# Sliding-window attention beside a gated feed-forward layer: the values' weights on ScalarE's queue, the order of early loads, and chunk 3's softmax in one group

## The chip, the cores and the metric

The kernel runs on one core of a Trainium2 chip. A core has TensorE (matmuls, PE in the profile; PEld is its loading of weights), VectorE (DVE), ScalarE (ACT), GpSimd (POOL) and SyncE (SP). SyncE, ScalarE and GpSimd can issue transfers, each on a queue of its own. The metric is the device time in microseconds (us) of one execution; lower is better.

## The reference

x has 2048 rows of 640 bf16 numbers. A layer normalization (no learned parameters) gives xn; two branches read it and their outputs are added to x:

```
xn = (x - mean(x)) / sqrt(var(x) + 1e-5)
# A: 32 heads of 20; each position s sees s, s-2, ..., s-14 (8 keys, dilation 2)
q, k, v = split(xn @ wqkv)
attn    = softmax(q . k[s - 2w] * 20**-0.5  over w = 0..7, masked where s - 2w < 0)
A       = (sum over w of attn[w] * v[s - 2w]) @ wo
# B: gated, without a nonlinearity
B       = ((xn @ w_gate) * (xn @ w_up)) @ w_down      # 640 -> 1536 -> 640
out     = x + A + B
```

## The kernel before

**Tiles and chunks.** The 2048 rows are 16 tiles of 128 rows, in four chunks of 512 rows. For each chunk the kernel makes xnT (the normalized x transposed, so that TensorE can contract over the 640 columns), q, k and v, the attention, the gate and up products, and the down projection. TensorE does the projections (line 464 by tiles of 128 rows, in chunk 0 while x is still arriving; line 500 by chunks), the gate and up products (L746), and down with the output projection of the attention (L809 for wd, L812 for wo). VectorE does the attention itself: products of q and k (L555), sums over the 20 numbers of a head in the `fold` steps (L530, L535), then, after TensorE has added up the last partial sums into logits with a matrix of ones and zeros (`logits`, L582, PSUM tile `pl`), the softmax (`softmax`: maximum L618, subtraction L622, sum L640, reciprocal L643, scaling L649; the exponential is ScalarE's, L632), and the weighted sum over v (`av`: products L698, sums L708 and L706, output tile oT). The softmax's weights go to device memory (aD, L658) and come back spread over the partitions (aE, four transfers a chunk, L666), each issued on SyncE's queue. VectorE also multiplies gate by up (hT, L763).

**Groups of the softmax.** `GR = (1, 1, 1, 2)` says in how many groups of positions each chunk's logits, softmax, store and spreading are done. In one group a chunk has eight logits matmuls, and its softmax works on 128x1024 numbers. Chunk 3 has two groups: four logits matmuls and half-sized operations for each, a store and four spreading transfers for each, and two half-sized products of L698 for each tile.

**Tiles 0 to 7.** Tiles 0 to 2 are transposed by TensorE (L385) and copied out by ScalarE (L390); from tile 3 on a transposing transfer on SyncE's queue does it (`transposes`, L379). Normalization of tiles 0 to 7: VectorE takes the statistics (L253, L259), GpSimd a power of -1/2 (L267, rstd), VectorE applies them (L272), in place in the x tile. There are five x buffers, so x of tile t+5 can be loaded only when tile t has been transposed. x of tile 8 is loaded by GpSimd's queue, right behind tile 3's transpose:

```
        if t + 5 < W:
            X[t + 5] = load((11.0, 11.5, 14.2)[t], load_x(t + 5), [a])
        elif t == 3 or 8 <= t < NT - 5:
            X[t + 5] = add("POOL", 6.0, load_x(t + 5, nc.gpsimd), [a], occ=0.45, kb=160)
```

**Weights.** wq comes in three loads on ScalarE's queue (lines 235 to 237), followed by x of tile 3. wk and wv come on SyncE's queue (L185). The order on SyncE's queue before: x0, x1, x2, wk, x4, x5, x6, x7, tile 3's transpose, wv, the transposes of tiles 4 to 7, wg, x9 to x12, wu, wd, wo. x8 is on GpSimd's queue, ahead of which GpSimd waits for tile 3's transpose.

**What sets the order.** Every piece of work is a `Step` in a `Plan`, with an engine, a planned cost, how long it occupies its engine (`occ`), and the steps that it depends on. `Plan.order` is a list scheduler: on each engine it takes, of the steps that are ready, the one whose latest start is earliest, and it writes the instructions in that order. `PACE` scales the planned costs of an engine. Dependences given to `add` and `load` steer the plan only; on the chip an instruction waits for data and buffers alone, and each engine runs its instructions in the order written. `load` makes a step on SyncE's queue behind the load before it, with an earliest planned landing. TensorE's steps are chained one behind the other in the order of the program text (`pe_main`), each waiting for the PSUM bank used six steps before; only the logits are slotted in where the plan has them ready (a `margin` of 0.9 in chunk 0, 1 elsewhere).

Of the kernel before, what the change touches and what calls it, by code (L numbers as in the profile page):

```python
# [9 lines left out]
ACT = mybir.ActivationFunctionType  # L10
# [22 lines left out]
class Plan:  # L33
# [1 line left out]

    LAG = 0.06
    RAW = 0.116
    PACE = {"DVE": 1.03, "ACT": 1.0}
    INORDER = ("DVE", "PE", "ACT")

    def __init__(self):
# [2 lines left out]
    def add(self, eng, cost, fn, deps=(), occ=None, after=(), kb=0):  # L44
        k = self.PACE.get(eng, 1.0)
        s = Step(eng, cost * k, fn, deps, None if occ is None else occ * k, after)
        s.kb = kb
        s.pace = k
        s.idx = len(self.steps)
        self.steps.append(s)  # L50
        return s
# [60 lines left out]
def kernel(  # L112
# [11 lines left out]
    nc = tc.nc  # L124
# [3 lines left out]
    S, D = x_flat.shape  # L128
# [3 lines left out]
    W = 8  # L132
# [6 lines left out]
    NT = S // P  # L139
# [16 lines left out]
    wv = const.tile([P, KT, D], BF, name="wv")  # L156
# [10 lines left out]
    add = plan.add  # L167
    T = {}

    def new(key, shape, dtype, tag, bufs, pool=None):  # L170
        t = (pool or sb).tile(shape, dtype, name=tag, tag=tag, bufs=bufs)
        T[key] = t
        return t


    def load_x(t, eng=None):
        def fn():
            x = new(("x", t), [P, D], BF, "x", 5)
            (eng or nc.sync).dma_start(out=x[:], in_=x_flat[t * P : (t + 1) * P, :])
        return fn  # L180

    X = {}

    def wload(dst, src, eng=None):
        return lambda: (eng or nc.sync).dma_start(out=dst[:], in_=src.rearrange("(i p) f -> p i f", p=P))  # L185
# [10 lines left out]
    def load(at, fn, deps=()):  # L196
        s = chain[0] = add("SP", 2.0, fn, deps, occ=0.45, after=[chain[0]])
        s.floor = at
        return s

    def part(r, lo, hi):
        src = A_wqkv[lo * P : hi * P, r * D : (r + 1) * D].rearrange("(i p) f -> p i f", p=P)
        return lambda: nc.scalar.dma_start(out=WT[r][:, lo:hi, :], in_=src)  # L203
# [31 lines left out]
    WP = []  # L235
    for lo, hi, at in ((0, 1, 4.4), (1, 3, 5.1), (3, KT, 5.5)):
        WP.append(add("ACT", at, part(0, lo, hi), [C0], occ=0.48, after=WP[-1:]))
    X[3] = add("ACT", 5.2, load_x(3, nc.scalar), occ=0.45, after=[WP[2]])
    TB = add("ACT", 1.6, table, after=[X[3]])

    def warm():
# [34 lines left out]
    XT, TT, GL, RS = {}, {}, {}, {}  # L276
# [3 lines left out]
    def behind(s, a):  # L280
        s.after.append(a)
        s.deps.append(a)
        plan.steps.remove(s)
        plan.steps.append(s)
# [5 lines left out]
    def st_in(t, g, d=None):  # L290
        return inline("DVE", 0.48, ln_stats(t, g), [d or X[t]], 0.395)
# [5 lines left out]
    def apply_in(t):  # L297
        XT[t] = inline("DVE", 0.443, ln_apply(t), [RS[t]], 0.4)
# [57 lines left out]
    def pe_main(cost, fn, deps=(), banks=1):  # L356
        nonlocal main
        waits = []
        for k in range(banks):
            if len(ring) + k >= 6:  # L360
                waits.append(ring[len(ring) + k - 6])
        main = add("PE", cost + 0.165, fn, [main, *waits, *deps], occ=cost)
        return main
# [6 lines left out]
    def transposes(t):  # L370
        c, q = divmod(t, CH)

        def slot():
            if q == 0:
                new(("xnT", c), [P, KT, CS], BF, "xnT", XB)

        def dma():
            slot()
            nc.sync.dma_start_transpose(out=T["xnT", c][:, :, q * P : (q + 1) * P], in_=T["x", t][:])  # L379

        def piece(g0, g1, n):
            def pe():
                ps = new(("pst", t, n), [P, KT, P], BF, "ps", 6, psum)
                for g in range(g0, g1):
                    nc.tensor.transpose(ps[:, g, :], T["x", t][:, g * P : (g + 1) * P], ident[:])  # L385

            def ev():
                if n == 0:
                    slot()
                nc.scalar.copy(T["xnT", c][:, g0:g1, q * P : (q + 1) * P], T["pst", t, n][:, g0:g1, :])  # L390
            return pe, ev

        if t in PIECES:
            for n, (g0, g1) in enumerate(PIECES[t]):
                p, e = piece(g0, g1, n)
                w = g1 - g0
                a = pe_main(w * 0.056, p, [XT.get((t, n), XT[t])])
                a = add("ACT", 0.16 + w * P / 1200, e, [a, TT.get(t)], occ=0.07 + w * P / 1200)
                TT[t] = a
                TX.setdefault(t, []).append((g0, g1, a))  # L400
                ring.append(a)
            if t:
                behind(PV[t - 1][0], TT[t])
        else:
            if c < 2:
                a = TT[t] = chain[0] = add("SP", 3.0, dma, [XT[t]], occ=1.28, after=[chain[0]])
            else:
                a = TT[t] = add("SP", 2.8, dma, [XT[t], GP.get(c - XB)], occ=1.28, kb=200)
        if t + 5 < W:
            X[t + 5] = load((11.0, 11.5, 14.2)[t], load_x(t + 5), [a])  # L410
        elif t == 3 or 8 <= t < NT - 5:
            X[t + 5] = add("POOL", 6.0, load_x(t + 5, nc.gpsimd), [a], occ=0.45, kb=160)

    LL = {}
    GR = (1, 1, 1, 2)
    PV = {}
    R = {}
    PROJ = ("q", "k", "v")
# [12 lines left out]
    def halo(c, r):  # L431
# [10 lines left out]
        else:  # L442
            w = LL.get((c - 2, GR[c - 2] - 1)) if r == 1 else O16.get(CH * (c - 1) - 1)
            HALOCP[r, c] = add("ACT", 0.25, fn, [w, *R[r, c - 1]])
# [10 lines left out]
    def tile_part(r, t, n, g0, g1, deps):  # L455
        c, q = divmod(t, CH)
        j0, j1 = JS[n]

        def pe():
            if g0 == 0:  # L460
                new(("psv", r, t, n), [P, 512], F32, "ps", 6, psum)
            for j in range(j0, j1):
                for i in range(g0, g1):
                    nc.tensor.matmul(T["psv", r, t, n][:, (j - j0) * P : (j - j0 + 1) * P], lhsT=lhs(r, i, j),  # L464
                                     rhs=T["xnT", c][:, i, q * P : (q + 1) * P], start=(i == 0 and j == j0), stop=(i == KT - 1),
                                     skip_group_check=True)

        ws = WQ[: (1, 2, 2, 3, 3)[g1 - 1]] if r == 0 else WW[r]
        return pe_main((g1 - g0) * (j1 - j0) * 0.056, pe, [*deps, *ws], banks=1 if g0 == 0 else 0)
# [16 lines left out]
    def proj_tile(r, t, ns=(0, 1)):  # L486
        for n in ns:
            a = None
            for g0, g1, x in TX[t] if n == 0 and t in TX else [(0, KT, TT[t])]:
                a = tile_part(r, t, n, g0, g1, [x])  # L490
            tile_evict(r, t, n, a)

    def proj(c, r, lo=0, n=CS):
        for j in range(KT):
# [11 lines left out]
            ts = range(c * CH + lo // P, c * CH + (lo + n) // P)  # L506
            old = LL.get((c - 2, GR[c - 2] - 1)) if r < 2 else O16.get(CH * (c - 1) - 1)
            a = pe_main(KT * (n / 2400 + 0.0027), pe, [*WW[r], *[TT[t] for t in ts], old])
            e = add("ACT", 0.16 + n / 1200, ev, [a, HALOCP.get((r, c)), R.get((r, c - 2), [None])[0]], occ=0.07 + n / 1200)
# [54 lines left out]
    before = {}  # L564
    order = [(c, g) for c in range(NCH) for g in range(GR[c])]
    for a, b in zip(order, order[1:]):
        before[b] = a

    def logits(c, g):
        n = (c, g)  # L570
        E = CS // 4 // GR[c]

        def lg():
            if g == 0:
                new(("lps", c), [P, 2 * CS], F32, "pl", 1, psum)
            l = T["lps", c][:, g * W * E : (g + 1) * W * E].rearrange("p (w s) -> p w s", w=W)
            sets = 3 - GR[c]
            for b in range(sets):
# [5 lines left out]

        took = 0.2 + 0.2195 * 2 / GR[c]
        folds = [FO[4 * c + u] for u in range(4) if GR[c] == 1 or u // 2 == g]
# [276 lines left out]
    a = st_in(0, 0)  # L863
    a = st_in(0, 1, a)
    aggr_in(0, a)
    a = st_in(1, 0)
    a = st_in(1, 1, a)
# [8 lines left out]
    halo(0, 1)  # L876
    halo(0, 2)
    transposes(0)
    a0 = [None, None]
    for k, (g0, g1, x) in enumerate(TX[0]):  # L880
        for n in range(2):
            if k == 2 and n == 1:
                a = st_in(2, 0, None)
                a = st_in(2, 1, a)
                apply_in(1)
                transposes(1)
                WV = None
            a0[n] = tile_part(0, 0, n, g0, g1, [x])
            if k == 2:
                tile_evict(0, 0, n, a0[n])  # L890
    aggr_in(2, a)
    proj_tile(0, 1, (0,))
    a = st_in(3, 0)
    a = st_in(3, 1, a)
# [4 lines left out]
    proj_tile(0, 2, (0,))  # L899
    apply_in(3)  # L900
    transposes(3)
    WV = load(14.6, wload(wv, A_wqkv[:, 2 * D : 3 * D]))
    WW = (WP, [WK], [WV])
    proj_tile(0, 2, (1,))
    proj(0, 1, 0, 3 * P)
    proj_tile(0, 3)
# [4 lines left out]
        ln(t)  # L911
        transposes(t)
    WL["g"] = load(28.5, wload(wg, B_w_gate))
    for t in range(9, 13):
        X[t] = load(30.0, load_x(t), [TT[t - 5]])
    WL["u"] = load(36.0, wload(wu, B_w_up))
    proj(0, 2)
# [68 lines left out]
```

## Time and profile before

| | us |
|---|---|
| median of 3 runs | 258.23 (257.91 to 258.67) |
| profiled execution | 258.23 |
| its span, first to last instruction | 256.5 |
| TensorE busy | 251.8 (98%) |
| VectorE busy | 223.5 (87%) |
| ScalarE busy | 129.1 (50%) |
| GpSimd busy | 41.8 (16%) |
| transfers | 24.65 MB, 96 GB/s over the span |

The granted TensorE clock was 1.000. A row of the time-ordered view has: start in us, length in us, engine, line, operation, output tile and input tile, number of instructions, and in brackets the idle time of the engine just before and what ended it. Rows merge neighbouring instructions of one kind. Engine names with a q (SPq, ACTq) are the issuing of transfers; a transfer's own time to landing stands in the view of transfers, as the last number of a line. A row of the chain that ended last has: start, length, and the work that was on the chain then.

### The profile page before, as it was taken

To read this page: it belongs to the slowest core of one execution; us is meant where nothing else is said; L and a number is where in the kernel's file an instruction comes from. 1 tells how busy PE (TensorE), PEld (TensorE's weight loads), DVE (VectorE), ACT (ScalarE), POOL (GpSimd) and SP (SyncE) were. 2 spreads that over 40 slices of the span, in tenths; PEclk is the share of its full clock that TensorE was granted. 3 is DMA by queue.
4 is the path that set the end of the run, shared out by engine and by line. 5 is a ranking of instruction groups with operands and counts; after the bars stand their busy time and mean duration, and the time that the engine had idled before them with its cause. 6 is when DMAs were issued, how large, how long until landed. Compare 5 with 4: busy or idle time off the path is not lost.

```text
span 256.5 us, 3786 instructions
## 1 busy us (share of the span) xinstructions
PE 251.8 (98%) x1481; PEld 141.4 (55%) x1481; DVE 223.5 (87%) x273; ACT 129.1 (50%) x250; POOL 41.8 (16%) x61
## 2 busy tenths in 40 slices
PE   7999999999999999999999999999999999999995
PEld 2885554444456775444455766444457754445763
DVE  5769999997999999999999999799999999994011
ACT  2656689786589164655554114545542135554100
POOL 2432000411100711004100112000293120000110
PEclk9999999999999999999999999999999999999999
DMA  6895999058500278051400132520005534000221
GB/s 216 259 192 105 399 391 335 3 152 179 157 0 3 27 95 85 7 191 44 170 0 0 17 38 27 145 88 0 0 3 127 130 31 102 23 0 3 24 27 51
DMA packets 21953, 24.65 MB, mean 96 GB/s; under 512 B 10032, under 2 KB 18352, under 8 KB 21872
## 3 DMA queue, kind: packets, MB, share of 16 engines
q1 hardware_dynamic: 18672, 17.86, 24.0%
q0 software_dynamic: 2432, 5.57, 13.5%
q10 hardware_dynamic: 832, 0.98, 1.2%
q8 instruction: 11, 0.18, 0.3%
q14 instruction: 6, 0.05, 0.1%
HBM read 18.61 MB, written 5.96 MB: 96 GB/s over the span
## 4 chain that ended last, share of the span: by engine, by line
PE 96%; DMA 2%; ACTq 0%; DVE 0%; issue 0%
PE ps L746 40%; PE ps L500 23%; PE ps L809 20%; PE ps L812 8%; PE ps L464 3%; DMA wq<-in_A_wqkv_dram 2%; PE pl L582 1%; ACTq L203 0%; PE ps L385 0%; DVE x L820 0%; DVE gs L214 0%; DVE mhalf L216 0%; DVE dm L189 0%
## 5 line engine op out<-in xcount | busy, mean ns | idle before, releaser
L746 PE MATMUL ps<-xnT,wg 128*128 128x512 bf16 x240 | 59.7, 379 | 0.0
L746 PE MATMUL ps<-xnT,wu 128*128 128x512 bf16 x240 | 59.6, 379 | 0.0
L809 PE MATMUL ps<-wd,hT 128*128 128x320 bf16 (+2 forms) x384 | 57.4, 299 | 0.0
L698 DVE TENSOR_TENSOR av<-v,aE 128x5120 bf16<-128x5120 bf16 (+1 forms) x20 | 45.6, 2286 | 3.7 <-DMA aE<-aD 3.7
L809 PEld LDWEIGHTS <-hT 128*128 128x128 bf16 x384 | 37.0, 98 | 16.3 <-issue 0.7
L555 DVE TENSOR_TENSOR pw<-qk 128x2560 bf16<-128x2560 bf16 x28 | 40.8, 1485 | 0.1
L746 PEld LDWEIGHTS <-wu 128*128 128x128 bf16 x240 | 23.5, 98 | 28.3
L746 PEld LDWEIGHTS <-wg 128*128 128x128 bf16 x240 | 23.3, 98 | 28.1 <-issue 0.5
L751 ACT CAST us<-ps 128x512 bf16<-128x512 f32 x48 | 28.1, 585 | 21.2 <-PE ps L746 20.2
L751 ACT CAST gs<-ps 128x512 bf16<-128x512 f32 x48 | 28.1, 585 | 20.4 <-PE ps L746 20.3
L708 DVE TENSOR_TENSOR av<-av 128x2560 bf16<-128x2560 bf16 (+1 forms) x32 | 36.9, 1153 | 0.2
L824 ACT COPY y<-ps 128x320 f32<-128x320 f32 x28 | 11.5, 426 | 42.6 <-PE ps L812 32.7
L853 POOL DMA_DIRECT2D out_dram<-y x14 | 12.2, 871 | 105.3 <-ACT y L824 86.7
L812 PE MATMUL ps<-wo,oT 128*128 128x320 bf16 (+2 forms) x160 | 27.0, 299 | 0.0
L504 ACT CAST qk<-ps 128x512 bf16<-128x512 f32 (+1 forms) x35 | 19.9, 569 | 12.2 <-PE ps L500 12.2
L530 DVE TENSOR_TENSOR pw<-pw 128x2048 bf16<-128x2048 bf16 (+1 forms) x28 | 25.6, 951 | 0.0
L500 PE MATMUL ps<-xnT,wv 128*128 128x512 bf16 x100 | 22.3, 379 | 0.0
L763 DVE TENSOR_TENSOR hT<-gs,us 128x512 bf16<-128x512 bf16 x48 | 19.7, 417 | 2.5 <-ACT us L751 2.3
L500 PE MATMUL ps<-xnT,wk 128*128 128x512 bf16 (+1 forms) x100 | 20.9, 366 | 0.0
L812 PEld LDWEIGHTS <-oT 128*128 128x128 bf16 x160 | 15.5, 98 | 6.3
L790 POOL COPY gate<-hT 1x1 bf16<-1x1 bf16 x4 | 10.6, 2652 | 51.2 <-DVE hT L763 51.2
L500 PEld LDWEIGHTS <-wv 128*128 128x128 bf16 x100 | 11.6, 118 | 9.7 <-issue 0.4
(67 smaller groups left out, 200.8 us busy)
## 6 DMA issues: line engine op xcount, KB each, us to landing
aE<-aD SPq DMA_DIRECT2D x12, 256.0 KB, 4.0
out_dram<-y POOLq DMA_DIRECT2D x14, 160.0 KB, 3.8
wg<-in_B_w_gate_dram SPq DMA_DIRECT2D x1, 1920.0 KB, 9.1
wu<-in_B_w_up_dram SPq DMA_DIRECT2D x1, 1920.0 KB, 13.0
wd<-in_B_w_down_dram SPq DMA_DIRECT2D x1, 1920.0 KB, 17.9
out_dram<-in_A_x_dram POOLq DMA_DIRECT2D x3, 640.0 KB, 4.2
x<-in_A_x_dram SPq DMA_DIRECT2D x11, 160.0 KB, 5.3
aE<-aD SPq DMA_DIRECT2D x8, 128.0 KB, 2.6
```

Source lines behind the costliest of these rows:

```text
L500: nc.tensor.matmul(T[key][:, 0:n], lhsT=lhs(r, i, j), rhs=T["xnT", c][:, i, lo : lo + n], start=(i == 0), stop=(i == KT - 1))
L504: nc.scalar.copy(where(r, c, j, j + 1, lo, n)[:, 0, :], T[key][:, 0:n])
L530: nc.vector.tensor_tensor(w[:, :, lo:hi, :], w[:, :, lo:hi, :], w[:, :, a:b, :], ALU.add)
L555: nc.vector.tensor_tensor(o, qh, kh, ALU.mult)
L698: nc.vector.tensor_tensor(o, v, w, ALU.mult)
L708: nc.vector.tensor_tensor(v[:, 0:k], v[:, 0:k], v[:, k : 2 * k], ALU.add)
L746: nc.tensor.matmul(ps[:], lhsT=(wu if r else wg)[:, i, f * P : (f + 1) * P], rhs=T["xnT", c][:, i, :], start=(i == 0), stop=(i == KT - 1))
L751: nc.scalar.copy(s[:], T[key][:])
L763: nc.vector.tensor_tensor(h[:], T["gs", c, f][:], T["us", c, f][:], ALU.mult)
L809: nc.tensor.matmul(ps, lhsT=T["hT", c, f][:, q * P : (q + 1) * P], rhs=wd[:, f, sl], start=(f == 0), stop=(f == FT - 1 and not wo_part))
L812: nc.tensor.matmul(ps, lhsT=T["oT", t][:, g, :], rhs=wo[:, g, sl], start=False, stop=(g == KT - 1 and f1 == FT))
L853: nc.gpsimd.dma_start(out=out_flat[t * P : (t + 1) * P, :], in_=T["y", t][:], accum_op=ALU.add)
```

## The change

1. The pace of VectorE in the plan goes from 1.03 to 1.02, and the planned cost of x3's load from 5.2 to 5.0.
2. wv's load moves from SyncE's queue to ScalarE's, planned after the normalization of tile 3 (`XT[3]`).
3. On SyncE's queue x7 moves from the place behind tile 2's transpose to behind tile 3's transpose.
4. x8 moves from GpSimd's queue (behind tile 3's transpose) to SyncE's, between wg and x9.
5. Chunk 3's softmax goes in one group: `GR` is (1, 1, 1, 1).

wq's three loads stay. The order on SyncE's queue after: x0, x1, x2, wk, x4, x5, x6, tile 3's transpose, x7, the transposes of tiles 4 to 7, wg, x8 to x12, wu, wd, wo.

```diff
--- before.py
+++ after.py
@@ -35,7 +35,7 @@
 
     LAG = 0.06
     RAW = 0.116
-    PACE = {"DVE": 1.03, "ACT": 1.0}
+    PACE = {"DVE": 1.02, "ACT": 1.0}
     INORDER = ("DVE", "PE", "ACT")
 
     def __init__(self):
@@ -235,7 +235,7 @@
     WP = []
     for lo, hi, at in ((0, 1, 4.4), (1, 3, 5.1), (3, KT, 5.5)):
         WP.append(add("ACT", at, part(0, lo, hi), [C0], occ=0.48, after=WP[-1:]))
-    X[3] = add("ACT", 5.2, load_x(3, nc.scalar), occ=0.45, after=[WP[2]])
+    X[3] = add("ACT", 5.0, load_x(3, nc.scalar), occ=0.45, after=[WP[2]])
     TB = add("ACT", 1.6, table, after=[X[3]])
 
     def warm():
@@ -406,13 +406,13 @@
                 a = TT[t] = chain[0] = add("SP", 3.0, dma, [XT[t]], occ=1.28, after=[chain[0]])
             else:
                 a = TT[t] = add("SP", 2.8, dma, [XT[t], GP.get(c - XB)], occ=1.28, kb=200)
-        if t + 5 < W:
-            X[t + 5] = load((11.0, 11.5, 14.2)[t], load_x(t + 5), [a])
-        elif t == 3 or 8 <= t < NT - 5:
+        if t < 2:
+            X[t + 5] = load((11.0, 11.5)[t], load_x(t + 5), [a])
+        elif 8 <= t < NT - 5:
             X[t + 5] = add("POOL", 6.0, load_x(t + 5, nc.gpsimd), [a], occ=0.45, kb=160)
 
     LL = {}
-    GR = (1, 1, 1, 2)
+    GR = (1, 1, 1, 1)
     PV = {}
     R = {}
     PROJ = ("q", "k", "v")
@@ -884,7 +884,6 @@
                 a = st_in(2, 1, a)
                 apply_in(1)
                 transposes(1)
-                WV = None
             a0[n] = tile_part(0, 0, n, g0, g1, [x])
             if k == 2:
                 tile_evict(0, 0, n, a0[n])
@@ -899,8 +898,9 @@
     proj_tile(0, 2, (0,))
     apply_in(3)
     transposes(3)
-    WV = load(14.6, wload(wv, A_wqkv[:, 2 * D : 3 * D]))
+    WV = add("ACT", 5.4, wload(wv, A_wqkv[:, 2 * D : 3 * D], nc.scalar), [XT[3]], occ=0.48)
     WW = (WP, [WK], [WV])
+    X[7] = load(14.6, load_x(7), [TT[2]])
     proj_tile(0, 2, (1,))
     proj(0, 1, 0, 3 * P)
     proj_tile(0, 3)
@@ -911,7 +911,7 @@
         ln(t)
         transposes(t)
     WL["g"] = load(28.5, wload(wg, B_w_gate))
-    for t in range(9, 13):
+    for t in range(8, 13):
         X[t] = load(30.0, load_x(t), [TT[t - 5]])
     WL["u"] = load(36.0, wload(wu, B_w_up))
     proj(0, 2)
```

## The prediction

> **What bounds the kernel now.** I read the page first, then the chain that ended last, then the time-ordered rows from 5 to 45 us, where most of the edits lie, and the VectorE rows from 160 us on, for chunk 3.
>
> ```profile
> span 256.5 us, 3786 instructions
> PE 251.8 (98%) x1481; PEld 141.4 (55%) x1481; DVE 223.5 (87%) x273; ACT 129.1 (50%) x250; POOL 41.8 (16%) x61
> ...
> 2.17 5.82 DMA wq<-in_A_wqkv_dram
> ...
> 10.36 2.01 PE ps L464 x35
> 12.37 4.06 PE ps L500 x25
> 16.43 2.79 PE ps L464 x50
> 19.22 21.58 PE ps L500 x100
> 40.81 0.64 PE pl L582 x8
> ...
> 166.15 0.33 PE pl L582 x4
> ...
> 206.49 0.33 PE pl L582 x4
> ```
>
> TensorE is busy 251.8 of 256.5 us. After the last load of wq has landed (2.17 + 5.82 = 7.99) each piece of the chain starts where the one before ends, to 253.6. So any edit after 8 us can win only TensorE work that it removes, and loses one for one where it makes TensorE wait. Nothing in the diff changes the loads ahead of 8 us. The profiled execution took 258.23 us, equal to the median of the three runs: 1.73 us lie outside the span.
>
> The second thing to see is how little slack the early rows have:
>
> ```profile
> 11.11 1.31 SPq L379 DMA_TRANSPOSE xnT<-x  x1
> 12.48 1.92 SPq L185 DMA_DIRECT2D wv<-in_A_wqkv_dram  x1
> 14.50 8.47 SPq L379 DMA_TRANSPOSE xnT<-x  x4
> 15.86 0.76 POOL L179 DMA_DIRECT2D x<-in_A_x_dram  x1 [2.39 <-DMA xnT<-x]
> 16.11 1.56 PEld L464 LDWEIGHTS <-wq 128*128 128x128 bf16 x25
> 16.64 0.57 POOL L267 TENSOR_TENSOR rstd<-ve,mhalf 128x1 f32<-128x1 f32 x1
> 17.26 0.45 DVE L272 TENSOR_SCALAR x<-x,mv,rstd 128x640 bf16<-128x640 bf16 x1 [2.18 <-POOL rstd L267]
> 19.06 5.56 PE L500 MATMUL ps<-xnT,wv 128*128 128x512 bf16 x25
> 24.45 5.56 PE L500 MATMUL ps<-xnT,wq 128*128 128x512 bf16 x25
> ...
> xnT<-x SPq DMA_TRANSPOSE x1, 4.4
> ...
> wv<-in_A_wqkv_dram SPq DMA_DIRECT2D x1, 800.0 KB, 6.4
> ```
>
> The last two lines are from the view of transfers: the transpose of tile 3 lands 4.4 us after its issue (11.11 + 4.4 = 15.5) and TensorE's weights for that tile load at 16.11: slack 0.6 us. wv lands at 12.48 + 6.4 = 18.9, wanted at 19.06. The transpose of tile 7, alone at the end of its four, takes 2.6 us from 21.77 and lands at 24.4, wanted at 24.45. And GpSimd, waiting for tile 3's transpose to issue x8, holds up the rstd of tile 5 (ready at 14.28, run at 16.64) and so VectorE by 2.18 us.
>
> **wv on ScalarE's queue.** Its issue costs ScalarE 0.40 to 0.49 us (the three rows of wq). The planner places it when tile 3's normalization is planned to end (11.09 in the trace); there ScalarE has just finished copying tile 2's transposes (10.28 to 11.03). The evictions behind it slip 0.45 us; TensorE does not feel that, since six PSUM banks of 0.56 to 0.86 us each lie between an eviction and the matmul that reuses its bank, and ScalarE idles 0.33 to 0.44 us ahead of each of the next evictions. If the issue came ahead of tile 2's copies it would cost 0.45 us; I take 0. wv itself, issued 1 us sooner, lands by 11.5 + 6.4 = 17.9 at the latest row: hidden. wv has no wait of its own on the chip, since nothing used its buffer before.
>
> The price is elsewhere. Before, wv's bytes moved after the transpose of tile 3, on the same queue (from 16 to 19 us, at 300 to 385 GB/s: 2.1 us for 800 KB). Now they are in flight beside it. Rows for a transpose: alone 2.6 us; with GpSimd's accumulating store beside it 5.7 and 4.8 (issued at 93.75 and 95.07, the two ahead of them 2.6); tile 3's own, with no other data queue beside it, 4.4, because its packets on one engine came only from 14.05 to 14.75, behind a fetch of instructions that began at 12.56. Lower end 2.6: lands at 13.7, no wait. Upper end 4.4 + 2.1 = 6.5: lands at 17.6, a wait of 1.5. I take 5.4, between the two rows with another queue beside them: lands at 16.5, TensorE waits 0.3 to 0.4. The Trainium skill ("DMA: Bandwidth & Descriptors", issuing engines are not separate DMA queues) says that transfers from different issuers share the same 16 engines and interleave. The trace agrees: x tile 0, ahead of the wq loads, lands in 2.2 us, and tiles 1 and 2 beside them in 3.3 and 5.1. The same skill ("Advanced Engine Details and Errata", X-Bar transpose) gives transposes nearly the speed of plain copies, 350 to 400 GB/s; by that an estimate for tile 3's 160 KB is 0.45 us of transfer, it would be through before wv's bytes start, and the sum would lose its 0.3. The trace disagrees: tile 7's, undisturbed, moves from 22.95 to 23.75, 200 GB/s.
>
> **Tile 3's transpose ahead of x7.** Its issue waits for tile 3's normalization (ends 11.09), and x7's issue was over at 10.71; so it still starts at 11.11 and its first packets follow some 1.15 us later as tile 7's do: 0 gained. x7 is issued at 12.45 in place of 10.39 and lands 2.2 to 5.5 us later (the quickest and slowest x loads up to here), 14.7 to 18.0. VectorE reads it at 17.92 in the old order. So at worst 0.1 us later, which tile 7's transpose (slack 0.1) would hand on; I take 0. With wv gone from SP's queue, tile 4's transpose can be issued at 14.0 in place of 14.50.
>
> **x8 on SP's queue.** GpSimd is free at 14.28, so tile 5 is normalized up to 2.2 us sooner, and tiles 6 and 7 as far as x7 allows. What this moves is VectorE, not TensorE: 0 by itself, and a cushion for tile 7. x8 is now issued behind wg, at about 23.7; the x9 issued there takes 8.9 us, so x8 lands near 32.5. ScalarE reads x8 at 31.61, and would wait 0.9 with evictions queued behind it; the six banks, now of 1.08 us each, cover that. wu, behind 160 KB more (0.4 us at 400 GB/s), lands at 25.83 + 13.0 + 0.4 = 39.2; the first wu matmul is at 42.46: hidden. Its issue adds about 0.5 us on SP ahead of wu, wd and wo, inside the same 3 us.
>
> **Chunk 3 in one group.** TensorE: two groups of four logits matmuls, 0.33 + 0.33, become one of eight, 0.54 to 0.64 in the other chunks: -0.1 us, the only work removed. VectorE before and after, per operation:
>
> ```profile
> 192.16 0.68 DVE L618 TENSOR_REDUCE m<-pl 128x64 f32<-128x512 f32 x1
> ...
> 203.08 1.28 DVE L535 TENSOR_TENSOR qk<-pw 128x1024 bf16<-128x1024 bf16 x2
> ...
> 151.62 1.22 DVE L618 TENSOR_REDUCE m<-pl 128x128 f32<-128x1024 f32 x1
> ...
> 167.03 2.83 DVE L698 TENSOR_TENSOR av<-v,aE 128x5120 bf16<-128x5120 bf16 x1 [2.07 <-DMA aE<-aD]
> ```
>
> Five softmax operations cost 0.68 + 0.70 + 0.68 + 0.55 + 0.69 = 3.30 twice, 6.6, against 1.22 + 1.23 + 1.22 + 0.95 + 1.23 = 5.85; eight products of 1.48 (11.8) become four of 2.83 (11.3). VectorE saves 1.2 us, off the path. But all attention weights of the chunk now wait for its last half. The last sum (204.36) loses 3.30 of softmax and 2.89 of products in front of it, some 201.1 to 204.4; take the logits at 204.2. In chunk 2, logits to weights took 151.02 to 160.02 (9.0) and weights to first product 160.04 to 167.03 (7.0): first product at 220.2. There the four outputs followed after 6.4, 15.7, 22.0 and 25.2 us: 226.6, 235.9, 242.2, 245.4. TensorE wants them at 236.33, 241.22, 245.84 and 251.58; the least slack is 3.6 us. Cost 0; if the cover is gone, one for one beyond 3.6.
>
> **Planner numbers.** The pace of 1.02 and x3's 5.0 change only the order in which steps are written. TensorE's own order is fixed but for the logits. In chunk 1 the last sum ends at 95.34 and the logits start at 96.71, in chunk 2 at 147.49 and 151.0; in chunk 0 there is no slack (the last sum ends at 41.00, during its logits, which take 0.64 and not 0.54). I take 0; bounds -0.1 (chunk 0's 0.1 back) and +1.0 (below).
>
> **Sum.** 256.5 - 0.1 + 0.3 = 256.7, with 1.73 outside 258.4 us. A change under 0.3% (0.8 us) is about what a measurement of this kernel cannot tell from none.
>
> **Rivals.** (1) *Tile 3 pays in full.* wv and the transpose start together and the engine that was late is late by wv's share too; TensorE stands 0.9 to 1.5 us at 16.4. For it: a slack of 0.6 and 5.7 us in a neighbouring row; against it, those rows are mostly shorter than 6. It decides from a landing of 6.0 us (17.1) on: 256.5 - 0.1 + 1.2 + 1.73 = 259.3. (2) *The logits come a step too early.* The planner now takes VectorE for 1% quicker; over the 54 us before chunk 1's logits that is 0.5 us against steps of 2.3, a chance of about one in five that they move one step, to 94.4, where they wait 1.0 for the sums; chunk 0's could move by 1.08 with no slack at all: 259.2. (3) *Chunk 3's weights come late* by more than 3.6 us: 260 to 262. (4) *Faster by over 0.3%.* It needs 0.8 us; TensorE's waits on wq are 1.0 in all and no edit reaches them, the logits give 0.1 each at two places: about 257.4, for a shorter start that I can't name. (5) *The edits do nothing*: wv and tile 3 don't meet, 258.1; it lies within the forecast's own range.
>
> **How the numbers follow.** The forecast with (5), waits of 0 to 0.8 us: 0.55, its own range 258.0 to 259.0. (1) 0.24, (2) 0.11, (3) 0.06, (4) 0.04. Slower by over 0.3%: 0.24 + 0.11 + 0.06 = 0.41; same 0.55; faster 0.04. The range runs from 257.9 to 259.8: it leaves out (3), (4) and the tail of (1), under 2 in 10.
>
> **What would show it.** Tile 3's transpose lands between 15.5 and 17.6 and the first matmul on tile 3 has an idle time released by that transfer; GpSimd's rstd of tile 5 runs by 15; VectorE has no 2.18 us wait there; one group of eight logits near 204 us, VectorE's last output near 245. The prediction is wrong if the chain shows a wait on a sum ahead of logits, or on wv, tile 7's transpose or chunk 3's outputs.

## The result, and the profile after

| | before | after |
|---|---|---|
| median of 12 runs, us | 257.85 (257.31 to 260.25) | 259.57 (258.35 to 262.02) |
| profiled execution, us | 258.23 | 259.8 |
| its span, us | 256.5 | 257.7 |

The ratio of the two is 1.0070, with a 95% interval of 1.0049 to 1.0091: the change makes the kernel slower by 1.7 us. All ratios below are against the kernel before on the same chip.

The head of the page of the changed kernel and, from its fourth part, the share of the chain by engine:

```profile
span 257.7 us, 3750 instructions
...
PE 250.6 (97%) x1464; PEld 141.2 (55%) x1481; DVE 223.5 (87%) x264; ACT 128.9 (50%) x249; POOL 44.0 (17%) x60
...
PE 92%; DMA 4%; DVE 2%; issue 1%; POOL 0%; SPq 0%
```

TensorE is the bound as before, but a transfer now stands in its chain. (1464 against 1481 matmuls is no saving: 17 matmul records are missing from this trace, and the weight loads are 1481 in both.) From the chain, in order of time (start, length, what):

```profile
10.61 6.69 DMA xnT<-x
17.34 2.99 PE ps L464 x50
```

The transpose of tile 3 lands 6.69 us after its issue, and the tile's 50 matmuls begin at 17.34. The rows around it in the time-ordered view:

```profile
10.35 0.38 ACTq L185 DMA_DIRECT2D wv<-in_A_wqkv_dram  x1
10.61 1.31 SPq L379 DMA_TRANSPOSE xnT<-x  x1
11.59 4.23 PE L500 MATMUL ps<-xnT,wk 128*128 128x384 bf16 x25
12.02 0.59 SPq L179 DMA_DIRECT2D x<-in_A_x_dram  x1
14.16 0.55 POOL L267 TENSOR_TENSOR rstd<-ve,mhalf 128x1 f32<-128x1 f32 x1 [0.89 <-DVE ve L261]
17.34 1.59 PE L464 MATMUL ps<-xnT,wq 128*128 128x128 bf16 x25 [1.52 <-DMA xnT<-x]
17.79 0.89 DVE L253 BATCH_NORM_STATS2 st<-x 128x6 f32<-128x320 bf16 x2 [2.26 <-DMA x<-in_A_x_dram]
```

wv's load is issued 0.26 us ahead of the transpose, TensorE then stands 1.52 us for the transpose, and VectorE stands 2.26 us for x7. From the start of the projection with wk to tile 3, TensorE took 12.21 to 16.27 = 4.06 us before, and 11.59 to 17.34 = 5.75 us now (both in the time-ordered view): 1.69 us more, which is the whole difference of the medians (1.72). The spans differ by only 1.2 because wq's last load happened to take 5.8 us in the profiled execution of before and 4.7 in this one, so this one reached wk's projection 0.62 us sooner. The list of TensorE's waits holds no other new one: none on wv, on tile 7's transpose, on sums ahead of logits, or on chunk 3's outputs.

Why the transpose is so late is seen in the packets of the queues, in windows of half a microsecond, from the view of transfers. q10 is ScalarE's queue (wv), q1 SyncE's (here the transpose); a line gives packets, MB, and the share of 16 engines. The first window is 12.0 to 12.5, then 13.5 to 14.0 and 14.5 to 15.0:

```profile
q10 hardware_dynamic: 30, 0.04, 52.6%
...
q10 hardware_dynamic: 140, 0.18, 100.0%
...
q1 hardware_dynamic: 356, 0.09, 233.5%
q10 hardware_dynamic: 51, 0.05, 29.8%
```

From 12.0 to 14.0 q10 moves 30 + 95 + 132 + 140 = 397 packets and q1 not one. The transpose's small packets come only when wv's have nearly run out. In this trace the bytes of wv do not share with the transpose, they go ahead of it. The Trainium skill ("DMA: Bandwidth & Descriptors", issuing engines are not separate DMA queues) says that transfers of different issuers interleave. The first loads of x and wq do so in the trace of before: from 4.0 to 4.5 us q10 had 72 packets and q1 57. For the transpose, issued 0.26 us behind wv, this trace differs.

Chunk 3 on VectorE, time-ordered view:

```profile
203.22 1.23 DVE L618 TENSOR_REDUCE m<-pl 128x128 f32<-128x1024 f32 x1 [1.81 <-PE pl L582]
...
216.19 2.83 DVE L698 TENSOR_TENSOR av<-v,aE 128x5120 bf16<-128x5120 bf16 x1 [0.59 <-DMA aE<-aD]
...
240.87 0.49 DVE L706 TENSOR_TENSOR oT<-av 128x640 bf16<-128x640 bf16 x1
```

One softmax, products from 216.19, the last output written by 241.4, and no wait of TensorE behind it.

### The profile page after: what moved, and what is told of

It is laid out like the page before. It is cut to its first block, busy times and chain, and to the rows that moved or that the text cites. A ratio compares the mean times of both kernels' runs of the same rounds, so it can differ in the third digit from the quotient of the medians.

```text
span 257.7 us, 3750 instructions
## 1 busy us (share of the span) xinstructions
PE 250.6 (97%) x1464; PEld 141.2 (55%) x1481; DVE 223.5 (87%) x264; ACT 128.9 (50%) x249; POOL 44.0 (17%) x60
## 4 chain that ended last, share of the span: by engine, by line
PE 92%; DMA 4%; DVE 2%; issue 1%; POOL 0%; SPq 0%
PE ps L746 40%; PE ps L500 21%; PE ps L809 20%; PE ps L812 8%; DMA xnT<-x 3%; DMA x<-in_A_x_dram 1%; PE ps L464 1%; DVE st L253 1%; PE pl L582 1%; DVE x L272 1%; POOL rstd L267 0%; DVE ve L261 0%; SPq L179 0%; DVE mv L259 0%; DVE x L820 0%
## 5 line engine op out<-in xcount | busy, mean ns | idle before, releaser
L698 DVE TENSOR_TENSOR av<-v,aE 128x5120 bf16<-128x5120 bf16 x16 | 45.1, 2820 | 3.6 <-DMA aE<-aD 3.6
L790 POOL COPY gate<-hT 1x1 bf16<-1x1 bf16 x4 | 12.1, 3017 | 49.7 <-DVE hT L763 49.7
L812 PEld LDWEIGHTS <-oT 128*128 128x128 bf16 x160 | 15.5, 98 | 6.3
```

Source lines behind the costliest of these rows:

```text
L698: nc.vector.tensor_tensor(o, v, w, ALU.mult)
L812: nc.tensor.matmul(ps, lhsT=T["oT", t][:, g, :], rhs=wo[:, g, sl], start=False, stop=(g == KT - 1 and f1 == FT))
```

## The experiments

The first theory: the transpose of tile 3 waits for wv's bytes, so the loss is wv's alone and is gone when wv is issued behind the transpose. The rivals: the loss comes from x7's or x8's new place, or from chunk 3's group. The medians, all in us:

| kernel | what stands | median (runs) | before, same chip | ratio (95%) | tile 3's transpose lands after |
|---|---|---|---|---|---|
| the change | all | 259.57 (12) | 257.85 | 1.0070 (1.0049 to 1.0091) | 6.7 |
| wv_only | wv's load alone | 261.66 (6) | 257.64 | 1.0149 (1.0124 to 1.0173) | 6.4 |
| wv_back | x8, group, pace | 257.51 (12) | 257.64 | 1.0003 (0.9990 to 1.0016) | 3.9 |
| wv_late | all, wv behind the transpose | 260.06 (4) | 257.64 | 1.0099 (1.0086 to 1.0112) | 3.6 |
| wv_part | all, 2/5 of wv ahead | 258.45 (11) | 257.64 | 1.0032 (1.0015 to 1.0048) | 5.5 |
| x8_back | all but x8 | 261.13 (6) | 257.64 | 1.0130 (1.0092 to 1.0168) | 6.4 |
| x7_back | all but x7 | 261.33 (6) | 257.64 | 1.0130 (1.0084 to 1.0177) | 6.3 |
| wv_late_x7 | wv_late and x7 back | 258.12 (12) | 257.64 | 1.0009 (0.9990 to 1.0028) | 4.9 |
| group_only | chunk 3's group alone | 258.25 (12) | 257.72 | 1.0013 (0.9991 to 1.0035) | |
| t3_pe | all, tile 3 by TensorE | 258.66 (12) | 257.72 | 1.0029 (1.0006 to 1.0052) | none |

The ratio and its interval come from the rounds of runs, so the quotient of the two medians can differ from it by up to 0.1%.

**wv's load alone.** The kernel before with only this edit; the instructions of TensorE, VectorE and GpSimd are those of before.

```diff
-    WV = load(14.6, wload(wv, A_wqkv[:, 2 * D : 3 * D]))
+    WV = add("ACT", 5.4, wload(wv, A_wqkv[:, 2 * D : 3 * D], nc.scalar), [XT[3]], occ=0.48)
```

> The kernel before with one edit: wv's load goes from SyncE's queue to ScalarE's. TensorE's, VectorE's and GpSimd's instructions are those of before, in the same order. Theory: the loss is the wait for tile 3's transpose behind wv's bytes, and this edit alone brings it. In the changed kernel wv was issued at 10.35 and the transpose at 10.61; here the plan puts wv one eviction later, at about 11.8, after the transpose's issue at 11.11. If the two transfers share the engines whatever their order, the transpose lands at 16 to 17.5 and the kernel takes 0.5 to 1.7 us more than before (258.4 to 259.6). If the one issued first goes first, the transpose lands near 15.5 and the time stays at 257.9. Rival (the loss comes from the other edits): also 257.9, but with the transpose landing late in the trace.

Measured: 261.66, more than twice the loss of the whole change. wv was issued at 10.18 and the transpose at 10.44, so wv went first here too (the expectation had assumed the other order). The execution that was profiled is the quickest of the six (259.75); its time-ordered view:

```profile
16.88 1.59 PE L464 MATMUL ps<-xnT,wq 128*128 128x128 bf16 x25 [1.18 <-DMA xnT<-x]
...
17.14 0.76 POOL L179 DMA_DIRECT2D x<-in_A_x_dram  x1 [3.34 <-DMA xnT<-x]
17.92 0.57 POOL L267 TENSOR_TENSOR rstd<-ve,mhalf 128x1 f32<-128x1 f32 x1
...
25.70 0.60 PE L500 MATMUL ps<-xnT,wq 128*128 128x512 bf16 x2 [0.44 <-ACT v L504]
```

It shows the wait at tile 3, and GpSimd, which still issues x8 behind the transpose, standing 3.34 us with the rstd of tile 5 queued behind. It also shows a second, shorter wait of TensorE, 0.44 us at 25.70, ended by ScalarE's eviction of v. This edit alone brings the loss, and the other edits of the change must take some of it back.

**wv back on SyncE's queue.** From the changed kernel, wv goes behind tile 3's transpose on SyncE's queue again and x7 ahead of it; x8's place, the single group and the pace of the plan stay.

```diff
-        if t < 2:
-            X[t + 5] = load((11.0, 11.5)[t], load_x(t + 5), [a])
+        if t + 5 < W:
+            X[t + 5] = load((11.0, 11.5, 14.2)[t], load_x(t + 5), [a])
...
-    WV = add("ACT", 5.4, wload(wv, A_wqkv[:, 2 * D : 3 * D], nc.scalar), [XT[3]], occ=0.48)
+    WV = load(14.6, wload(wv, A_wqkv[:, 2 * D : 3 * D]))
...
-    X[7] = load(14.6, load_x(7), [TT[2]])
```

> The changed kernel with wv's load back on SyncE's queue behind tile 3's transpose, and x7 back ahead of that transpose; x8 on SyncE's queue, chunk 3 in one group and the planner's numbers stay changed. Theory: the wait of 1.5 us at tile 3 goes; 257.85 - 0.1 for the logits = 257.7 (257.4 to 258.0). Rival (another edit costs): 258.5 or more, with another wait of TensorE in the trace.

Measured: 257.51, as expected, and no difference from before (1.0003). The transpose lands after 3.9 us, and TensorE goes on to tile 3 without idle time:

```profile
xnT<-x SPq DMA_TRANSPOSE x1, 3.9
...
15.38 1.56 PE L464 MATMUL ps<-xnT,wq 128*128 128x128 bf16 x25
```

TensorE waits for no transfer later on either. x8, the group and the pace together are worth nothing that can be measured, neither gain nor loss, as long as the transpose is on time.

**Chunk 3's group alone,** on the kernel before: `GR = (1, 1, 1, 1)`.

> The kernel before with one edit: chunk 3's softmax in one group. By the prediction's step it removes 0.1 us of TensorE's work and costs nothing else, since the least slack of chunk 3's outputs is several us: 257.4 to 257.8 beside 257.6 for before. Rival (all of chunk 3's weights wait for its last half): 258.5 or more, with TensorE waiting for an output of chunk 3.

Measured: 258.25 against 257.72, between the expectation and the rival, but with a ratio of 1.0013 whose interval holds 1. TensorE waits for no output of chunk 3, so its weights are not late. The 0.1 us of logits is below what these runs tell apart.

**wv still on ScalarE's queue, but behind the transpose.** In the plan wv's load now stands behind tile 2's projection with wk (`PV[2][1]`); everything else is as in the change.

```diff
     transposes(3)
-    WV = add("ACT", 5.4, wload(wv, A_wqkv[:, 2 * D : 3 * D], nc.scalar), [XT[3]], occ=0.48)
-    WW = (WP, [WK], [WV])
     X[7] = load(14.6, load_x(7), [TT[2]])
     proj_tile(0, 2, (1,))
+    WV = add("ACT", 5.4, wload(wv, A_wqkv[:, 2 * D : 3 * D], nc.scalar), [XT[3]], occ=0.48, after=[PV[2][1]])
+    WW = (WP, [WK], [WV])
```

> The changed kernel with wv still on ScalarE's queue but issued about 1.8 us later, behind ScalarE's eviction of tile 2 (about 12.2 in place of 10.35), so after the transpose's issue at 10.6 and after its first packets (11.8). All other instructions keep their order. If the first to be issued goes first: the transpose lands by 14 to 15.5, no wait at tile 3, wv lands by 18.5, and the time is 257.5 to 257.9. If both share the engines whatever their order: the transpose lands at 15.5 to 16.5, 257.9 to 258.6. If wv's late landing is wanted at 19: a wait there of up to 0.5.

Measured: the mechanism as expected, the time not. The transpose was issued at 10.45, wv at 11.68. The packets, from 12.0 to 12.5, 12.5 to 13.0 and 13.0 to 13.5:

```profile
q1 hardware_dynamic: 329, 0.08, 256.8%
...
q1 hardware_dynamic: 22, 0.01, 25.1%
...
q10 hardware_dynamic: 45, 0.06, 66.4%
q1 hardware_dynamic: 146, 0.03, 32.3%
```

Now the transpose is ahead: it lands after 3.6 us, and TensorE starts tile 3 at 15.53 without a wait. x7 now has the place that the transpose had: a plain load on q1, issued at 11.87, 0.19 us behind wv. From 12.0 to 13.5 q1 moves the transpose's small packets, and from 13.5 to 15.5 the view of transfers has one queue only:

```profile
q10 hardware_dynamic: 529, 0.68, 97.3%
```

So x7 too moves nothing until wv has nearly run out, 1.5 us past the landing of the transpose (14.0). The order is not shown to be a matter of transposing transfers alone.

And still the kernel took 260.06. The time-ordered view, early and at chunk 2's projections:

```profile
17.10 0.89 DVE L253 BATCH_NORM_STATS2 st<-x 128x6 f32<-128x320 bf16 x2 [2.00 <-DMA x<-in_A_x_dram]
...
62.67 1.24 SPq L379 DMA_TRANSPOSE xnT<-x  x1
...
69.02 2.33 PE L500 MATMUL ps<-xnT,wq 128*128 128x512 bf16 x10 [2.39 <-issue]
```

The loss has moved 50 us down. x7, issued behind the transpose, lands late, and VectorE stands 2.00 us for it. Chunk 0's softmax follows later (its maximum at 43.20, against 41.06 where x7 was early, in wv_back), then the store of its weights (52.50 against 50.72). SyncE's queue takes that store and three of the four spreading transfers ahead of chunk 2's last transpose, so this one is issued at 62.67 (against 60.88) and lands 6.3 us later (against 4.3), at 69.0, when TensorE has stood 2.39 us for it. The profile calls the releaser "issue"; we take it to be this transfer, because its landing and the start of the projection agree to 0.1 us. The late issue is only half of the account. In the kernel before, the same transpose is issued at 62.29, hardly sooner, but takes 3.1 us, and TensorE doesn't wait. Here GpSimd issues two loads of x beside it (63.04 and 63.95, against 63.75 and 64.52 before); whether these make it take 6.3 us is not shown.

**The same with x7 back ahead of the transpose** is the test of that reading.

> The kernel with the later issue of wv (behind tile 2's eviction), and x7 back ahead of tile 3's transpose. There the transpose landed in time, but x7, queued behind it and beside wv, was read at 17.1, and TensorE waited 1.8 us at 67 us for chunk 2's transposes. Theory: x7's late landing delays VectorE, with it the softmax of chunk 0 and the transposes queued behind its transfers; with x7 early again this wait goes: 257.4 to 258.0. Rival (wv beside the transposes is what costs, whatever x7 does): 259 or more.

Measured: 258.12, ratio 1.0009: the loss is gone. In the time-ordered view:

```profile
15.65 1.56 PE L464 MATMUL ps<-xnT,wq 128*128 128x128 bf16 x25
15.88 0.88 DVE L253 BATCH_NORM_STATS2 st<-x 128x6 f32<-128x320 bf16 x2
...
66.86 5.34 PE L500 MATMUL ps<-xnT,wq 128*128 128x512 bf16 x24
```

No idle time at tile 3, none for x7, none at chunk 2 (its last transpose is issued at 61.29 and lands after 5.1 us). That x7's place decides about the wait at chunk 2 is shown by this pair of kernels; the path through VectorE and SyncE's queue is read from the traces. So the change has two costs: the wait at tile 3, and a late x7 that would cost at chunk 2. They don't add up. In the changed kernel TensorE reaches chunk 2's projections at 68.47, and the last transpose of chunk 2 lands at 63.16 + 5.2 = 68.4, just in time, because TensorE had already lost 1.5 us at tile 3.

**Two fifths of wv ahead of the transpose.** 320 KB go where the change puts wv, the other 480 KB on SyncE's queue behind x7.

```diff
-    WV = add("ACT", 5.4, wload(wv, A_wqkv[:, 2 * D : 3 * D], nc.scalar), [XT[3]], occ=0.48)
-    WW = (WP, [WK], [WV])
+    WVa = add("ACT", 5.4, part(2, 0, 2), [XT[3]], occ=0.48)
     X[7] = load(14.6, load_x(7), [TT[2]])
+    wv_rest = A_wqkv[2 * P : D, 2 * D : 3 * D].rearrange("(i p) f -> p i f", p=P)
+    WVb = load(15.0, lambda: nc.sync.dma_start(out=wv[:, 2:KT, :], in_=wv_rest))
+    WW = (WP, [WK], [WVa, WVb])
```

> The changed kernel with two fifths of wv (320 KB) at wv's place on ScalarE's queue and three fifths (480 KB) on SyncE's queue behind x7. Theory: the transpose waits for the bytes ahead of it, so its delay falls with them: of the 2.1 us of wv some 0.85 are left, the transpose lands near 15.5 to 16, the wait at tile 3 is 0 to 0.5, and the time is 257.7 to 258.3 if the rest of wv lands before 19. Rival (a fixed price for any load ahead of a transpose): the wait stays at 1.5 us and the time at 259.3 or more.

Measured: 258.45, slightly above the expected range. The two transfers that meet (issued at 10.08 and 10.35), and TensorE's wait at tile 3 and at chunk 2:

```profile
wv<-in_A_wqkv_dram ACTq DMA_DIRECT2D x1, 320.0 KB, 5.1
xnT<-x SPq DMA_TRANSPOSE x1, 5.5
...
15.91 1.59 PE L464 MATMUL ps<-xnT,wq 128*128 128x128 bf16 x25 [0.36 <-DMA xnT<-x]
...
67.52 4.70 PE L500 MATMUL ps<-xnT,wq 128*128 128x512 bf16 x21 [0.49 <-DMA xnT<-x]
```

The landing goes with the bytes ahead: 3.6 to 4.9 us with none (wv_back, wv_late, wv_late_x7), 5.5 with 320 KB, 6.3 to 7.6 with 800 KB (7.6 in the second trace of wv_only, below). The two waits together, 0.85, make up the loss of 0.81.

**x8 alone back on GpSimd's queue,** the rest of the change standing.

```diff
-        elif 8 <= t < NT - 5:
+        elif t == 3 or 8 <= t < NT - 5:
...
-    for t in range(8, 13):
+    for t in range(9, 13):
```

> The changed kernel with x8 alone back on GpSimd's queue, where GpSimd waits for tile 3's transpose before it goes on to the rstd of tile 5; TensorE's, VectorE's and ScalarE's instructions stay as they are. Theory: the late transpose costs twice where GpSimd also waits for it, because tiles 5 to 7 are then normalized late too and the projections of chunk 1 wait; so x8's move saves in the changed kernel what makes the kernel with wv's move alone 2 us slower than it: 261 to 262. Rival (x8's queue does not matter, VectorE's order or the group is what differs): 259.6, as the changed kernel.

Measured: 261.13, as expected, and some 1.6 us above the change; the intervals of the two ratios lie just apart. The time-ordered view:

```profile
17.70 0.76 POOL L179 DMA_DIRECT2D x<-in_A_x_dram  x1 [3.90 <-DMA xnT<-x]
...
19.09 0.45 DVE L272 TENSOR_SCALAR x<-x,mv,rstd 128x640 bf16<-128x640 bf16 x1 [3.69 <-POOL rstd L267]
...
70.20 2.14 PE L500 MATMUL ps<-xnT,wq 128*128 128x512 bf16 x9 [0.92 <-DMA xnT<-x]
```

The late transpose holds GpSimd 3.90 us, so VectorE 3.69 us, and TensorE pays once more, 0.92 at chunk 2 and 0.45 at 26.27, 1.4 in all. Moving x8 off GpSimd's queue is worth some 1.6 us once the transpose is late, and nothing that can be measured when it is on time (wv_back).

**x7 alone back ahead of the transpose,** wv staying where the change has it (in code the x7 part of wv_back's diff).

> The changed kernel with x7 alone back ahead of tile 3's transpose. Theory: the transpose waits for wv's bytes whether x7 stands ahead of it or not; 259.2 to 259.9, a wait of 1.2 to 1.9 us at tile 3. Rival (x7 behind the transpose is a second cost, as the late read of x7 at 17.1 to 17.8 suggests): 258.5 or less.

Measured: 261.33, worse than either theory had it. Three runs took 259.93 to 260.60 and three 262.05 to 263.24; the latter three had a mean granted TensorE clock of 0.993, the former 0.999 to 1.000. The profiled execution (259.93) waits 1.02 us at tile 3, behind a start that was itself 1.2 us late for wq; the two together, 2.2, are nearly its whole loss of 2.3. So x7's order doesn't mend the wait at tile 3, and the clock comes into play.

**wv's load alone, a second trace,** with the kernel of the first experiment.

> The kernel before with wv's move alone, once more for its trace: the profiled execution, 259.75, was the quickest of six, the others took 261.1 to 262.2. Theory: a typical execution shows a second wait of TensorE of some 2 us beside the one at tile 3, either at chunk 1's first projection (24 to 26 us), since GpSimd waits for the same transpose, or at chunk 2's (67 us). Rival: the wait at tile 3 itself is 3 us or more.

Measured: 261.87, at a mean clock of 0.993. The time-ordered view, and then the table by stretches (from 19 to 20 and from 20 to 21 us; the granted clock is the third number from the end):

```profile
18.23 2.19 PE L464 MATMUL ps<-xnT,wq 128*128 128x128 bf16 x25 [2.48 <-DMA xnT<-x]
20.22 2.63 PE L464 MATMUL ps<-xnT,wk 128*128 128x128 bf16 x25
```

```profile
19.00:20.00 1.00, 1.00 (x13) 1.00 (x11) 0.12 (x1) 0.48 (x1) 0.83 (x2) 0.52 0.08 20
20.00:21.00 1.00, 1.00 (x12) 1.00 (x11) 0.97 (x5) 0.37 (x1) 0.29 (x1) 0.50 0.49 143
```

The transpose took 7.6 us to land and TensorE stood 2.48 us; then the clock was halved until about 22.4, and tile 3's 50 matmuls took 18.23 to 22.68 = 4.45 us in place of 2.8: 1.7 us more. Neither theory was right: in this execution the loss of 4.2 us is a longer wait at tile 3 and the clock, and there is no second wait further down. The Trainium skill ("TensorE: Matmul & The Clock Gate", Part 1: the HAM clock gate) tells of a gate that knows only full and half speed, judges by a free-running window of about 3.4 us, and so turns at a moment that differs from run to run. The half speed agrees with this trace's 0.50. The clock fell at 19.0, 0.8 us after the end of a wait of 2.48 us; that the wait was the cause is inferred. The wait of 2.39 us in wv_late left the clock at 1.00.

**Tile 3 transposed by TensorE,** in the changed kernel, so that no transposing transfer stands behind wv until tile 4.

```diff
-    PIECES = {0: ((0, 1), (1, 3), (3, 5)), 1: ((0, 1), (1, 3), (3, 5)), 2: ((0, 3), (3, 5))}
+    PIECES = {0: ((0, 1), (1, 3), (3, 5)), 1: ((0, 1), (1, 3), (3, 5)), 2: ((0, 3), (3, 5)), 3: ((0, 3), (3, 5))}
```

> The changed kernel, wv still ahead on ScalarE's queue, but tile 3 is transposed by TensorE and copied out by ScalarE like tiles 0 to 2, so that no transposing transfer stands behind wv's bytes until tile 4's. It adds five transposes to TensorE (0.28 us). Theory (the wait is tile 3's transpose alone): no wait at 16 us, 257.5 + 0.3 = 257.8, up to 258.4 where tile 4's transposes or x7 come late. Rival (wv on that queue delays more than tile 3): 259 or more, with a wait of TensorE at 19, 25 or 67 us.

Measured: 258.66 against 257.72 before, a loss of 0.9 in place of 1.7, above what the theory expected and below the rival's 259. Tile 3 is not waited for at its projection. Two of TensorE's waits from the list (total, times, longest), and the rows of its transposes of tile 0 and of tile 3:

```profile
PE ps L385 <- DVE x L272: 0.9, 1, 0.9
PE ps L500 <- issue: 0.2, 1, 0.2
...
5.76 0.80 PE L385 MATMUL ps<-ident,x 128*128 128x128 bf16 x5 [0.87 <-DVE x L272]
...
10.97 0.44 PE L385 MATMUL ps<-ident,x 128*128 128x128 bf16 x5
```

So about half of the loss is regained. The wait of 0.9 us stands at tile 0, at 5.76, where the kernel before starts too (5.80); tile 3's transposes start without one. What this version pays is five more transposes (0.28 us in its chain) and 0.2 us at chunk 2's projections (67.18). That makes 0.5 of the 0.9; where the rest lies is not shown, and the interval of the ratio runs from 0.15 to 1.3 us. No version beat the kernel before.

## Why the prediction was right or wrong

It forecast no measurable difference, 258.4, and gave 0.24 to what came, its first rival: tile 3 pays in full, 259.3. The measured time is 259.57: within the range, because the range was made to reach into that rival, but outside the likeliest case's own range (258.0 to 259.0). The mechanism was named rightly, the choice between its sizes was not, and that the time falls near the forecast is partly luck (see the base, below).

- **The wait at tile 3 is the term of the sum that was mis-sized:** 0.3 taken from a landing of 5.4 us; measured 6.69 and 1.5 (1.7 counted from wk's projection). It was taken between two rows of a transpose that has a store beside it, as if wv and the transpose shared the engines. The runs show an order: of wv and the transpose, what was issued first goes first. The upper end of the bounds (6.5, a wait of 1.5) was this case, worked out and then not chosen.
- **Who is issued first was not worked out.** The prediction placed wv when ScalarE had copied tile 2's transposes, at 11.03, and the transpose at 11.11, and called that together. On the chip the order was wv first by 0.16 to 0.26 us in the traces of the change, wv_only, x8_back and x7_back, and the order decides: 1.2 us the other way (wv_late) removes the wait. How small a lead is enough was not tried.
- **The issue on ScalarE** at 0: no wait of TensorE behind it. wv landed at 10.35 + 6.3 = 16.7, before 17.9 as said, and is wanted at 20.17.
- **Tile 3's transpose ahead of x7** at 0: right in the changed kernel, by a cover that the prediction didn't name. x7 landed at 17.7, inside 14.7 to 18.0, although it took longer (5.7 us) than the slowest load that the prediction counted (5.5; x3's, on ScalarE's queue, had taken 5.7). VectorE, made earlier by x8's move, waited 2.26 us for it. Of who waits for VectorE the prediction looked at tile 7's transpose alone; the price stands at chunk 2's transposes, behind chunk 0's softmax on SyncE's queue, and was 2.4 us where TensorE was not late already (wv_late).
- **x8 on SyncE's queue** at 0, "a cushion": right without the late transpose (wv_back), and with it worth some 1.6 us (x8_back). The rstd of tile 5 ran at 14.16, by 15 as said; ScalarE read x8 at 32.72 in an unbroken row of evictions.
- **Chunk 3 in one group** at -0.1: no wait, as said (group_only), with more room than worked out: logits at 202.62 for 204.2, products at 216.19 for 220.2, last output at 241.4 for 245.4. (The products of 2.89 us at 204.28 in the trace of before stand behind the last sum, not in front of it as the prediction has it; the bounds that it gives for the logits are those of the softmax's 3.30 us alone, so nothing hangs on it.)
- **The plan's numbers** at 0: the logits moved to 41.91, 97.90 and 149.89. With TensorE some 1.1 us later there, this puts chunk 2's a step sooner, chunk 0's and 1's where they were. No trace shows a wait on sums; the second rival didn't come.
- **The base** was the profiled execution, 258.23; the median of 12 runs of before is 257.85, so the forecast sat 0.4 us high and seemed nearer to the result than its terms were.

Left open: five of the six runs of wv_only took 261.1 to 262.2, and only the two near 262.2 show the lower clock (0.993). Of those at full clock but 261.1 to 261.7 there is no trace. The second waits of x8_back (0.45 and 0.92) would be a way; of these the trace of wv_only at 259.75 has the first (0.44), and the other is not shown in wv_only. Why the transpose, and x7 in wv_late, yield to a load that another queue issued 0.2 us sooner, when the first loads of x and wq share, the runs don't show.

## What to carry to other kernels

Before a load is moved to another queue, look at which transfer is issued within a microsecond of it, and in which order: here the transpose issued 0.2 us behind a load of 800 KB paid nearly all of that load's time, not a share of it. A wait that is removed can uncover another one further down that it had covered (here 50 us later), so undo the parts of a change in pairs too, not one at a time only. And of two edits, one can be worth nothing alone and some 1.6 us beside the other.

## What the runs showed of the hardware that was not expected

- A transposing transfer of 160 KB lands 3.6 to 4.9 us after its issue with no load ahead, 5.5 behind 320 KB and 6.3 to 7.6 behind 800 KB that another queue issued 0.16 to 0.27 us sooner. For 2 us (12.0 to 14.0 in the changed kernel) it moved no packet at all. A plain load behind the same load (x7 in wv_late) moved none from 13.5 to 15.5.
- TensorE's clock went to 0.50 after a wait of 2.48 us, for about 3.4 us, at a price of 1.7 us; after a wait of 2.39 us in another kernel it stayed at 1.00. Mean clocks of 0.993 appear in 1 of 12 runs of the change, 2 of the first 6 of wv_only, 3 of 6 of x7_back, 1 of 6 of x8_back and 1 of 12 of t3_pe, and in one of 23 runs of the kernel before (260.21). The traces of t3_pe and of the kernel before, both of runs at 1.000, show no wait of TensorE over 1.3 us, so a long wait is not shown to be the only way to the lower clock. What the lower clock costs, 1.7 us in the one run that was traced, is a part of the spread.
